# Value products cut into 64-key halves with two sums, and other work moved around the last slots

## The chip, the cores and the metric

The kernel runs on one core of one Trainium2 chip. The metric is the time of one execution on the device, in microseconds (us). The kernel before took 841.43 us (median of 3 runs, 840.59 to 842.06). The engines are called as in the profile: PE (matmul), PEld (its weight loads), DVE, ACT, POOL, and SP, which here only issues transfers (DMA).

## The reference

```python
def _A_ref(x, wqkv, wo):             # S = 2048, D = 512, H = 32, Dh = 16, W = 256
    q, k, v = ...                    # x @ wqkv, by heads
    scores = jnp.einsum("bhqd,bhkd->bhqk", q, k) * (Dh ** -0.5)
    mask = (idx[:, None] - idx[None, :] >= 0) & (idx[:, None] - idx[None, :] < W)
    p = _softmax(jnp.where(mask[None, None], scores, -1e9), axis=-1)
    o = jnp.einsum("bhqk,bhkd->bhqd", p, v)
    return o.reshape(B, S, D) @ wo   # after moving heads behind positions

def _B_ref(x, w_gate, w_up, w_down): # F = 1792
    return (_silu(x @ w_gate) * (x @ w_up)) @ w_down

g = _sigmoid((x * gate_w).sum(-1, keepdims=True))
return g * _A_ref(...) + (1 - g) * _B_ref(...)
```

Everything is float32. Each query sees itself and the 255 keys before it. The result is a gated mix of attention over that window and a feed-forward block (SwiGLU).

## The kernel before, in words

Large products are done as three products of split operands: a matrix is split into a rounded part and a rest (`split`, L64 to L67: the rounded part by ACT, POOL or DVE, the rest by POOL or DVE), and hi·hi, lo·hi and hi·lo are summed in PSUM. Scores use the split too; the value products (L320) are plain float32 and go through PE in two passes each.

The program is written out in order by hand (`manual_schedule`), so each engine executes its instructions in the order of the code. It has three stages.

*Start.* x is split, the value projection and the query and key projections of the first head group are done.

*Slots.* There are 8 groups of 4 heads and 16 blocks of 128 positions, so 128 slots `t`, and one more at the end (L524). A slot goes through four heads `hd`. For each, PE computes one score tile of the next group (L265), whose row maximum DVE takes (L267), and one score tile of this group (L302), which ACT exponentiates into `pt` (L304); POOL cuts the window's edges (L306, L309). Between them stand six matmuls of 64 rows (L216), two at a time in the upper and lower half of the array. They belong to *units*: four slots make a unit, which projects queries and keys of a later group or computes a tile of the gate and up products of the feed-forward block. Results go from PSUM (`pa`, `pb`, two buffers each) to SBUF by ACT copies (L474), and feed-forward tiles go on to DRAM (`raws`) by SP. A table `AT` puts further functions behind a head of a slot (`later`).

*In the first slot of a unit, at head 1*, comes `av`: the value products of the 512 queries `c` of a group that have just been completed. For each of up to six key blocks of 128 there are four products, one for each head, in four lanes of 32 columns; the `vg` tile is the weight (16 values and a column of ones), `pt` is streamed, and the lanes write four row groups of one PSUM tile (`pb`, at the end `pa`). Then `evac` transposes that tile in blocks of 32 on DVE (L330), and the generator `finish` divides by the sum (L336, L337), transposes back (L341) and writes to DRAM (`od`, issued by POOL), one step a slot at head 1. Just ahead of `av`, where a maximum of half a group is due, `put_max` transposes it on PE (L277), negates it on DVE (L279) and puts it into `QT`.

*The last group.* From slot 112 (`g7`) there are no scores of a next group, and so no maxima. There the gate sums of x · gate_w are done on DVE (L507), two blocks in each odd slot from 113, and down-projection weights are loaded and split for the first eight tiles (`wd_early`). The sigmoid's rest (L559 to L562) is done behind the slots.

*Down products.* For each of 4 column blocks `c` and 14 tiles `n`, `hidden` takes gate and up tiles back from DRAM (`load_kept`, L619 to L623, names `got`), applies SiLU on ACT and multiplies on DVE (L638); tile n = 1 is computed on PE instead (L634). `halved` splits the result into `hh` (ACT, L64) and `hl` (DVE, L67), and `step` does 12 matmuls (L82 to L84: three products for each of four accumulators `ps`). Further down weights are fetched and split on DVE eight tiles ahead, from n = 0 on. The attention's output projection and the mix stand among these steps.

What decides about memory: a pool that is opened later takes the SBUF of one that was closed, and the first transfer into it waits for every user of the old one.

Of the kernel before, what the change touches and what calls it, by code (L numbers as in the profile page):

```python
# [9 lines left out]
F32 = mybir.dt.float32  # L10
# [23 lines left out]
def gated_mix(ctx, tc, xT, xn, wqk, wv, wo, wgu, wd, gw, out):  # L34
# [43 lines left out]
    def mm3(ps, pairs, start=True, stop=True):  # L78

        n = len(pairs)  # L80
        for i, ((lh, ll), (rh, rl)) in enumerate(pairs):
            nc.tensor.matmul(ps, lh, rh, start=start and i == 0, stop=False)  # L82
            nc.tensor.matmul(ps, lh, rl, start=False, stop=False)  # L83
            nc.tensor.matmul(ps, ll, rh, start=False, stop=stop and i == n - 1)  # L84

    def run(gen, n=None):

# [77 lines left out]
    with ExitStack() as A:  # L165
# [107 lines left out]

        def put_max(g, hf):
            n = NB // 2
            pt = ps1.tile([P, CH], F32, name="ps1")
            nc.tensor.transpose(pt[:4 * n, :P], MX[g, hf].rearrange("p h b -> p (h b)"), ident)  # L277
            mt = sm.tile([4 * n, P], F32R, name="mt")
            nc.vector.tensor_scalar(mt, pt[:4 * n, :P], -1.0, None, op0=ALU.mult)  # L279
            for pr in range(2):  # L280
                nc.sync.dma_start(halves_of(QT[g % 2][pr])[hf][63::64].bitcast(F32),
                                  mt[2 * pr * n:2 * (pr + 1) * n].bitcast(F32))
# [30 lines left out]

        def av(g, c):

            AV[g, c] = pp.tile([P, CH], F32, name="pb" if 4 * g + c + 1 < len(UNITS) else "pa")
            for kb in range(max(0, 4 * c - 2), 4 * c + 4):
                b0, b1 = max(kb, 4 * c), min(kb + 3, 4 * c + 4)
                for j in range(4):
                    nc.tensor.matmul(AV[g, c][32 * j:32 * j + 32, (b0 - 4 * c) * P:(b1 - 4 * c) * P],  # L320
                                     VG[4 * g + kb // 4][:, kb % 4, 17 * j:17 * j + 32],
                                     PT[g, kb, j // 2][:, j % 2, (b0 - kb) * P:(b1 - kb) * P],
                                     start=kb == max(0, 4 * c - 2), stop=kb == 4 * c + 3, skip_group_check=True)

        OT = {}

        def evac(g, c):

            OT[g, c] = osb.tile([P, CH], F32, name="ot")
            nc.vector.transpose(OT[g, c], AV[g, c])  # L330

        def finish(g, c):

            v = OT[g, c].rearrange("p (s e) -> p s e", e=32)
            rc = osb.tile([P, CH // 32], F32, name="rc")
            nc.vector.reciprocal(rc, v[:, :, DH])  # L336
            nc.vector.tensor_tensor(out=v[:, :, :DH], in0=v[:, :, :DH],  # L337
                                    in1=rc[:, :, None].to_broadcast([P, CH // 32, DH]), op=ALU.mult)
            yield
            on = osb.tile([P, CH], F32, name="on")  # L340
            nc.vector.transpose(on, OT[g, c])  # L341
            yield
            nc.gpsimd.dma_start(od[g, :, c * CH:(c + 1) * CH], on)

        vp = ExitStack()
        vpool = vp.enter_context(tc.tile_pool(name="vpool", bufs=1))
        wvh = vpool.tile([P, NK, D], F32R, name="wvh")
        wvl = vpool.tile([P, NK, D], F32R, name="wvl")
        vs = [vpool.tile([P, G, 2, VW], F32, name=f"vs{i}") for i in range(2)]
# [102 lines left out]
        for n in range(4):  # L452
            load_v(n)
        vp.close()
        ptp = A.enter_context(tc.tile_pool(name="ptp", bufs=13))
        osb = A.enter_context(tc.tile_pool(name="osb", bufs=1))


        AT = {}

        def later(t, hd, *fs):
            AT.setdefault((t, hd), []).extend(fs)
# [1 line left out]
        def unit(key, t):  # L464


            later(t, 3, prepare)

            def done(hf):
                def copies(ps):  # L470
                    t0 = t + 3 + hf
                    places = [kept(), kept()]
                    for m in range(2):
                        later(t0, 2 * m, lambda m=m: nc.scalar.copy(places[m], ps[m]))  # L474
                    if key[0] == "f":
                        for m in range(2):
                            later(t0 + 1, 2, lambda m=m: nc.sync.dma_start(raws[key[1], key[2], 2 * hf + m], places[m]))
                        return
                    g = key[1]

                    def half(m):
                        if m == 0:
                            X[g, hf] = x_pair()
                        split_qk(g, hf, m, places[m])
                    t1 = t0 + 3 * hf
                    later(t1, 3, lambda: half(0))
# [23 lines left out]
        def wd_early(t, f, piece):  # L510
            later(t, 2, lambda: later(t + 1, 2, load_wd(f, piece, kept())))

        pieces = [h for two in (QT[0], KT[0], QT[1], KT[1]) for t in two for h in halves_of(t)]
        later(g7, 1, gate_place)
        for m in range(NB // 2):
            for b in (2 * m, 2 * m + 1):
                later(g7 + 2 * m, 1, lambda b=b: gate_fetch(b))
                later(g7 + 2 * m + 1, 3 * (b % 2), lambda b=b: gate_block(b))
            wd_early(g7 + 2 * m, ORDER[m], pieces[m])

        FIN, tops = iter(()), [(0, 1)]
        for t in range(G * NB + 1):  # L524
# [6 lines left out]
            for hd in range(4):  # L531
# [5 lines left out]
                run(turns[part], 3)  # L537
                for f in AT.pop((t, hd), ()):
                    f()
                if hd == 1 and part:  # L540
                    run(FIN, 1)
                if hd == 1 and part == 0:
                    while tops:
                        put_max(*tops.pop())
                    if t:
                        ag, c = divmod(d - 1, NCH)
                        av(ag, c)
                        evac(ag, c)
                        FIN = finish(ag, c)
            if i in (7, 15) and g + 1 < G:  # L550
                tops.append((g + 1, i // 8))
            if t >= 10 and t % 4 == 2 and t + 6 < G * NB:
                load_v((t + 6) // 4)
        prepare()
        run(FIN)
        for key in sorted(AT):
            for f in AT[key]:
                f()
        nc.scalar.activation(gate, gate, AF.Exp, scale=-1.0)  # L559
        nc.vector.tensor_scalar(gate, gate, 1.0, None, op0=ALU.add)  # L560
        nc.vector.reciprocal(gate, gate)
        nc.vector.tensor_scalar(igate, gate, -1.0, 1.0, op0=ALU.mult, op1=ALU.add)  # L562


    with ExitStack() as B:
        hp = B.enter_context(tc.tile_pool(name="hp", bufs=3))
        got = B.enter_context(tc.tile_pool(name="got", bufs=4))
# [26 lines left out]
        def attn_out(c, b, ohl):  # L594
# [4 lines left out]
            if c == 0:  # L599
                put(c, b, pa, gate)  # L600
            else:
                nc.scalar.activation(GA[:, b], pa, AF.Copy, scale=gate[:, t:t + 1])

        def put(c, b, ps, factor):

            t = 4 * c + b
            nc.vector.scalar_tensor_tensor(GA[:, b], ps, factor[:, t:t + 1], GA[:, b], op0=ALU.mult, op1=ALU.add)
            nc.sync.dma_start(out[0, t * P:(t + 1) * P], GA[:, b])

        def attn_step(c, b, hold={}):  # L610

# [5 lines left out]
        GOT = {}  # L617

        def load_kept(c, f):  # L619

# [23 lines left out]
            split(hh, hl, sg, nc.scalar, nc.vector)  # L644
            return c, n, hh, hl

        ACC = {}
        GA = by_k(slot("k11", F32))

        def step(c, n, hh, hl):  # L650

# [5 lines left out]
            if n == NF - 1:  # L657
                for b in range(4):
                    t = 4 * c + b
                    if c == 0:  # L660
                        nc.scalar.activation(GA[:, b], ACC[c][b], AF.Copy, scale=igate[:, t:t + 1])
# [4 lines left out]
        loads = [(c, ORDER[n]) for c, n in seq if n != 1]  # L666
        for _ in range(3):
            load_kept(*loads.pop(0))
        fresh, waiting, ready = [], [], []
        for c, n in seq:  # L670
            f = ORDER[n]
            todo, ready = ready, []
            if c == 0 and n < NF - 8:
                ready.append(load_wd(ORDER[n + 8], pieces[n + 8], raw2()))
            if c == 0 and n >= 6 and n % 2 == 0:
                ready.append(load_wo((n - 6) // 2))
            if n != 1 and loads:
                load_kept(*loads.pop(0))
            fresh.append((c, n, hidden(c, f)))
            for f in todo:  # L680
                f()
            while len(fresh) > (c + n > 0):
                waiting.append(halved(*fresh.pop(0)))
            if c == 0 and n >= NF - 4:
                load_oc(0, n - NF + 4)
            if c and 1 <= n < 5:
# [44 lines left out]
```

## Time and profile before

| what | value |
|---|---|
| median of 3 runs | 841.43 us (840.59 to 842.06) |
| the profiled execution's own time | 840.66 us |
| its span in the trace | 838.9 us |
| instructions | 18738 |
| value products (L320), matmul passes | 1408 |
| score exponentials (L304) | 512, mean 476 ns |
| score maxima (L267) | 512, mean 540 ns |
| end of slots, start of down products | about 608 to 618 us |

A row of a group reads: line, engine, operation, output <- inputs, partitions x elements, count | busy time in us, mean ns of one | idle time of the engine ahead of it, and what ended it. `128*32` is an array tile of 128 rows and 32 columns. A row of the chain of work reads: start in us, us, what. A row of the timeline reads: start, us, what, and in brackets the idle time ahead of it with its releaser. In a view of windows each engine's busy time and its count follow the length, then the granted PE clock, the share of the DMA engines and GB/s. PE matmuls overlap in the trace, so the mean of one is longer than its distance from the next.

### The profile page before, as it was taken

How to read it: one execution, taken by the hardware profiler on the slowest of the kernel's cores; microseconds unless marked ns; L12 is line 12 of the kernel's file. 1: busy time of each engine (PE TensorE's matmuls, PEld its weight loads, DVE VectorE, ACT ScalarE, POOL GpSimd, SP SyncE). 2: the span in 40 equal slices, each digit the busy share in tenths (PEclk: the TensorE clock that was granted, in tenths of full speed). 3: DMA queues.
4: the chain of work that ended last, by engine and by line, in shares of the span. 5: the costliest groups of instructions: out<-in, count | busy, mean ns of one | idle time of the engine just before them, and what ended most of it. 6: DMA issues, size and time to landing. Idle time of an engine off the chain costs nothing.

```text
span 838.9 us, 18738 instructions
## 1 busy us (share of the span) xinstructions
PE 829.5 (99%) x6934; PEld 682.2 (81%) x6934; DVE 504.9 (60%) x1380; ACT 433.9 (52%) x903; POOL 352.4 (42%) x638
## 2 busy tenths in 40 slices
PE   9999999999999999999999999999989999999998
PEld 7798878888878887887887788878858888888886
DVE  6396676677667666676677667746467353353443
ACT  6322656556656666566565665556544433243341
POOL 7712545455546555545554645456601111011020
PEclk9999999999999999999999999999999999999999
DMA  8573534625624533542552463456688444283451
GB/s 288 162 231 113 149 120 123 186 93 148 198 87 129 151 135 111 163 153 98 152 182 93 123 184 125 132 189 198 232 283 298 157 155 162 85 283 98 151 163 50
DMA packets 65996, 132.82 MB, mean 158 GB/s; under 512 B 9457, under 2 KB 14193, under 8 KB 65905
## 3 DMA queue, kind: packets, MB, share of 16 engines
q1 hardware_dynamic: 61936, 117.74, 44.6%
q0 software_dynamic: 3968, 13.90, 4.6%
q8 instruction: 54, 0.88, 0.4%
q14 instruction: 38, 0.30, 0.1%
HBM read 60.82 MB, written 45.35 MB: 127 GB/s over the span
## 4 chain that ended last, share of the span: by engine, by line
PE 96%; DMA 2%; SPq 1%; DVE 1%; issue 0%; ACT 0%
PE pb L216 24%; PE pa L216 23%; PE pb L320 9%; PE ps L84 6%; PE ps L265 6%; PE ps L82 6%; PE ps L83 6%; PE ps L302 5%; PE pb L196 2%; PE pa L196 2%; PE pb L84 2%; PE pb L83 2%; PE pb L82 2%; PE pb L634 1%; PE pa L634 1%; DMA raw<-wd 1%
## 5 line engine op out<-in xcount | busy, mean ns | idle before, releaser
L304 ACT ACTIVATE pt<-ps 128x384 f32<-128x384 f32 (+2 forms) x512 | 240.1, 476 | 210.6 <-PE ps L302 151.2
L267 DVE CUSTOM_DVE_ANT_0 ps<-ps,mask 128x384 f32<-128x384 f32 (+2 forms) x512 | 273.0, 540 | 90.3 <-PE ps L265 64.4
L306 POOL TENSOR_SCALAR_AFFINE_SELECT pt<-pt 128x256 f32<-128x256 f32 x256 | 113.8, 445 | 238.7 <-ACT pt L304 238.6
L302 PE MATMUL ps<-q,k 64*128 64x384 f32 (+2 forms) x512 | 160.2, 329 | 0.0
L265 PE MATMUL ps<-k,q 63*128 63x384 f32 (+2 forms) x512 | 159.0, 330 | 0.3 <-issue 0.3
L216 PE MATMUL pb<-xhi,wh 64*128 64x512 f32 x512 | 111.1, 394 | 0.0
L216 PE MATMUL pa<-xhi,wh 64*128 64x512 f32 x512 | 110.2, 393 | 0.0
L216 PE MATMUL pb<-xhi,wl 64*128 64x512 f32 x512 | 109.8, 389 | 0.0
L216 PE MATMUL pb<-xlo,wh 64*128 64x512 f32 x512 | 109.7, 390 | 0.0
L216 PE MATMUL pa<-xhi,wl 64*128 64x512 f32 x512 | 108.9, 390 | 0.0
L216 PE MATMUL pa<-xlo,wh 64*128 64x512 f32 x512 | 108.8, 390 | 0.0
L265 PEld LDWEIGHTS ps<-k,q 63*128 63x128 f32 x512 | 89.3, 184 | 13.7 <-issue 6.0
L302 PEld LDWEIGHTS ps<-q,k 64*128 64x128 f32 x512 | 89.3, 184 | 7.6 <-issue 0.8
L309 POOL TENSOR_SCALAR_AFFINE_SELECT pt<-pt 128x256 f32<-128x256 f32 x224 | 94.5, 422 | 0.0
L638 DVE TENSOR_TENSOR sg<-got,sg 128x512 f32<-128x512 f32 x52 | 44.0, 846 | 64.0 <-ACT sg L637 52.6
L320 PE MATMUL pb<-pt,vg 128*32 128x256 f32 (+2 forms) x1360 | 81.5, 386 | 0.0
L320 PEld LDWEIGHTS pb<-pt,vg 128*32 128x32 f32 x1360 | 40.1, 110 | 41.0 <-issue 21.4
L267 DVE DVE_READ_ACCUMULATOR2_ANT mx<- 128x1 f32 x512 | 72.2, 141 | 0.0
L330 DVE STREAM_TRANSPOSE ot<-pb 128x512 f32<-128x512 f32 x31 | 22.2, 717 | 77.7 <-PE pb L320 77.7
L216 PEld LDWEIGHTS pb<-xhi,wh 64*128 64x128 f32 x512 | 56.8, 185 | 7.4
L216 PEld LDWEIGHTS pb<-xhi,wl 64*128 64x128 f32 x512 | 56.9, 184 | 6.5
L216 PEld LDWEIGHTS pa<-xhi,wl 64*128 64x128 f32 x512 | 55.8, 184 | 7.0
(144 smaller groups left out, 1483.4 us busy)
## 6 DMA issues: line engine op xcount, KB each, us to landing
raws<-ev SPq DMA_DIRECT2D x104, 256.0 KB
got<-raws SPq DMA_DIRECT2D x104, 256.0 KB
od<-on POOLq DMA_DIRECT2D x32, 256.0 KB, 2.4
raw<-wgu SPq DMA_DIRECT2D x28, 256.0 KB
q<-xhi SPq DMA_DIRECT2D x56, 128.0 KB
k<-xhi SPq DMA_DIRECT2D x56, 128.0 KB
vd<-vs POOLq DMA_DIRECT2D x8, 672.0 KB, 4.5
vg<-vd SPq DMA_DIRECT2D x32, 168.0 KB
```

The costliest lines, as they stand in the source:

```text
L82: nc.tensor.matmul(ps, lh, rh, start=start and i == 0, stop=False)
L83: nc.tensor.matmul(ps, lh, rl, start=False, stop=False)
L84: nc.tensor.matmul(ps, ll, rh, start=False, stop=stop and i == n - 1)
L216: mm = nc.tensor.matmul(ps[me], w[r], x[r], start=not second and i == 0, stop=bool(second) and i == n - 1)
L265: nc.tensor.matmul(ps[:, :n], QT[g % 2][pr][r, q0:q0 + P], KT[g % 2][pr][r, k0:k0 + n], start=True, stop=True)
L267: mx = nc.vector.tensor_tensor_reduce(out=ps[:, :n], in0=ps[:, :n], in1=mask[:, 3 * P - n:], scale=1.0, scalar=NEG, op0=ALU.add, op1=ALU.m ...
L302: nc.tensor.matmul(ps[:, :n], KT[g % 2][pr][r, k0:k0 + P], QT[g % 2][pr][r, k0:k0 + n], start=True, stop=True)
L304: BEHIND.append(nc.scalar.activation(pt[:, j, :n], ps[:, :n], AF.Exp, scale=SCALE))
L306: nc.gpsimd.affine_select(out=pt[:, :, :P], in_=pt[:, :, :P], pattern=[[0, 2], [1, P]], compare_op=ALU.is_ge, fill=0.0, base=0, channel_mu ...
L309: nc.gpsimd.affine_select(out=pt[:, :, 2 * P:], in_=pt[:, :, 2 * P:], pattern=[[0, 2], [-1, P]], compare_op=ALU.is_ge, fill=0.0, base=-1, ...
L320: nc.tensor.matmul(AV[g, c][32 * j:32 * j + 32, (b0 - 4 * c) * P:(b1 - 4 * c) * P], VG[4 * g + kb // 4][:, kb % 4, 17 * j:17 * j + 32], PT ...
L638: nc.vector.tensor_tensor(out=sg, in0=gu[1], in1=sg, op=ALU.mult)
```

## The change

1. *Value products by halves of 64 keys.* `av` cuts each key block into its lower and upper 64 keys, and both have their own row half of the array: eight lanes of 64 rows and 32 columns. The sum over lower halves goes to `pb` (or `pa`), that over upper halves to a tile of `ps2`, or of `ps1` from the last group on. The blocks are taken in two orders so that both halves are equally wide in each round.
2. *Two sums.* `finish` copies the second sum on ACT, adds both on DVE, transposes, divides, transposes back and writes. Its first step stands behind `av`, the next behind head 2 of the same slot, the others behind head 1 of the next three slots. `evac` is gone.
3. `put_max` transposes in two halves, each into its own PSUM tile, by plain matmuls of 64 rows.
4. *Gate sums* start in slot 108, one behind head 2 and one behind head 3 of every odd slot; the sigmoid's rest stands in slot 125.
5. *The first tail tile* (c = 0, n = 0) is loaded in slot 124 and multiplied and split in slot 128, head 0, into half of `KT[1][1]`.
6. *Down rows* are loaded six tiles ahead, from n = 2 on, and their split stands behind `halved`.
7. The pools of value weights, `pt`, tail tiles (`hp`) and `got` are put on the right side of SBUF, and the ACT copies at the very end both stand at head 0.

```diff
         def put_max(g, hf):
             n = NB // 2
-            pt = ps1.tile([P, CH], F32, name="ps1")
-            nc.tensor.transpose(pt[:4 * n, :P], MX[g, hf].rearrange("p h b -> p (h b)"), ident)
             mt = sm.tile([4 * n, P], F32R, name="mt")
-            nc.vector.tensor_scalar(mt, pt[:4 * n, :P], -1.0, None, op0=ALU.mult)
+            for o in HALVES:
+                pt = ps1.tile([P, CH], F32, name="ps1")
+                nc.tensor.matmul(pt[:4 * n, :64], MX[g, hf].rearrange("p h b -> p (h b)")[o], ident[o, o],
+                                 start=True, stop=True)
+                nc.vector.tensor_scalar(mt[:, o], pt[:4 * n, :64], -1.0, None, op0=ALU.mult)
...
-            AV[g, c] = pp.tile([P, CH], F32, name="pb" if 4 * g + c + 1 < len(UNITS) else "pa")
-            for kb in range(max(0, 4 * c - 2), 4 * c + 4):
-                b0, b1 = max(kb, 4 * c), min(kb + 3, 4 * c + 4)
+            AV[g, c] = (pp.tile([P, CH], F32, name="pb" if 4 * g + c + 1 < len(UNITS) else "pa"),
+                        ps1.tile([P, CH], F32, name="ps1") if 4 * g + c + 1 >= 4 * (G - 1) else ps2.tile([P, CH], F32, name="ps2"))
+            orders = [[4 * c + m for m in ms if 4 * c + m >= 0] for ms in ((0, 1, 2, -1, -2, 3), (0, 1, -1, 2, 3, -2))]
+            for n, kbs in enumerate(zip(*orders)):
                 for j in range(4):
-                    nc.tensor.matmul(AV[g, c][32 * j:32 * j + 32, (b0 - 4 * c) * P:(b1 - 4 * c) * P],
-                                     VG[4 * g + kb // 4][:, kb % 4, 17 * j:17 * j + 32],
-                                     PT[g, kb, j // 2][:, j % 2, (b0 - kb) * P:(b1 - kb) * P],
-                                     start=kb == max(0, 4 * c - 2), stop=kb == 4 * c + 3, skip_group_check=True)
+                    for h, (o, kb) in enumerate(zip(HALVES, kbs)):
+                        k0 = kb * P + 64 * h
+                        q0, q1 = max(k0, c * CH), min(k0 + W + 64, c * CH + CH)
+                        nc.tensor.matmul(AV[g, c][h][32 * j:32 * j + 32, q0 - c * CH:q1 - c * CH],
+                                         VG[4 * g + kb // 4][o, kb % 4, 17 * j:17 * j + 32],
+                                         PT[g, kb, j // 2][o, j % 2, q0 - kb * P:q1 - kb * P],
+                                         start=n == 0, stop=n == len(orders[0]) - 1, skip_group_check=True)
...
         def finish(g, c):
-            v = OT[g, c].rearrange("p (s e) -> p s e", e=32)
+            first, second = AV[g, c]
+            if not AB:
+                AB.extend(osb.tile([P, CH], F32, name=f"o{n}") for n in range(2))
+            both, ot = AB[::-1] if c % 2 else AB
+            lo = 0 if c else 64
+            nc.scalar.copy(both[:, lo:], second[:, lo:])
+            yield
+            nc.vector.tensor_tensor(out=both[:, lo:], in0=first[:, lo:], in1=both[:, lo:], op=ALU.add)
+            if lo:
+                nc.vector.tensor_copy(both[:, :lo], first[:, :lo])
+            yield
+            nc.vector.transpose(ot, both)
+            yield
...
-        later(g7, 1, gate_place)
+        later(g7 - 4, 1, gate_place)
+        for b in range(NB):
+            t = g7 - 4 + b // 2 * 2
+            later(t, 1, lambda b=b: gate_fetch(b))
+            later(t + 1, 2 + b % 2, lambda b=b: gate_block(b))
+        later(g7 + NB - 3, 0, gate_end)
...
+        def tile0():
+            (gt, up), sg = [GOT.pop((ORDER[0], i, 0)) for i in range(2)], kept()
+            nc.scalar.activation(sg, gt, AF.Silu)
+            nc.vector.tensor_tensor(out=sg, in0=up, in1=sg, op=ALU.mult)
+            split(*TILE0, sg, nc.scalar, nc.vector)
+        later(g7 + NB - 4, 1, tile0_load)
+        later(g7 + NB - 1, 3, lambda: later(g7 + NB, 0, prepare, tile0))
...
-                if hd == 1 and part:
+                if (part, hd) in ((0, 2), (1, 1), (2, 1), (3, 1)):
                     run(FIN, 1)
...
                         av(ag, c)
-                        evac(ag, c)
                         FIN = finish(ag, c)
+                        run(FIN, 1)
...
-        fresh, waiting, ready = [], [], []
+        fresh, waiting, ready = [], [(0, 0, *TILE0)], []
...
-            if c == 0 and n < NF - 8:
-                ready.append(load_wd(ORDER[n + 8], pieces[n + 8], raw2()))
+            if c == 0 and 2 <= n < NF - 6:
+                ready.append(load_wd(ORDER[n + 6], pieces[n + 6], raw2()))
...
-            fresh.append((c, n, hidden(c, f)))
+            if c + n:
+                fresh.append((c, n, hidden(c, f)))
+            if len(fresh) > 1:
+                waiting.append(halved(*fresh.pop(0)))
             for f in todo:
                 f()
-            while len(fresh) > (c + n > 0):
-                waiting.append(halved(*fresh.pop(0)))
```

On PE, the value products of the second block of 512 queries of group 0 stood in this order (the line, the operation, out<-in, the columns of the array by the columns streamed):

```order
L216 MATMUL pa<-xhi_71,wl 128x512
L277 MATMUL ps_1559<-ident,mx 32x128
L320 MATMUL pb<-pt,vg 32x128 x4
L320 MATMUL pb<-pt,vg 32x256 x4
L320 MATMUL pb<-pt,vg 32x384 x8
L320 MATMUL pb<-pt,vg 32x256 x4
L320 MATMUL pb<-pt,vg 32x128 x4
L265 MATMUL ps_1592<-k_353,q_351 128x384
```

In the changed kernel the same place on PE begins and goes on as follows, with both sums in turn (eight rows of each width but 320, of which there are sixteen):

```order
L218 MATMUL pa<-xhi_71,wl 128x512
L281 MATMUL ps_1586<-ident,mx 32x64
L281 MATMUL ps_1589<-ident,mx 32x64
L330 MATMUL pb<-pt,vg 32x320
L330 MATMUL ps_1595<-pt,vg 32x320
...
L330 MATMUL pb<-pt,vg 32x256
...
L330 MATMUL pb<-pt,vg 32x192
...
L330 MATMUL pb<-pt,vg 32x64
...
L330 MATMUL pb<-pt,vg 32x128
L330 MATMUL ps_1595<-pt,vg 32x128
L267 MATMUL ps_1645<-k_353,q_351 128x384
```

The 24 products have become 48, each over 64 keys, and the widest is 320 instead of 384.

On DVE, behind those products, before (ISA is the score maximum and the reading of its result):

```order
L279 TENSOR_SCALAR mt<-ps_1559 32x128
L330 STREAM_TRANSPOSE ot<-pb 128x512
L267 ISA ps_1592,mx<-ps_1592,mask 128x384
L267 ISA mx 128x1
...
L336 RECIPROCAL rc<-ot 128x16
L337 TENSOR_TENSOR ot<-ot,rc 128x16x16
```

and with the change (`o` are the two tiles that `finish` uses in turn):

```order
L283 TENSOR_SCALAR mt<-ps_1586 32x64
L283 TENSOR_SCALAR mt<-ps_1589 32x64
L269 ISA ps_1645,mx<-ps_1645,mask 128x384
L269 ISA mx 128x1
L347 TENSOR_TENSOR o_1336<-pb,o_1336 128x512
```

The reader of `pb` has moved behind the maximum of the next head, and is an addition that also waits for ACT's copy.

Where the down products begin, DVE had this order before (`sg` SiLU times up, `hl` the rest of its split, `q` the place of a down-weight tile, `raw` the tile as loaded):

```order
L638 TENSOR_TENSOR sg_9873<-got1_9857,sg_9873 128x512
L67 TENSOR_TENSOR hl_9877<-sg_9873,hh_9876 128x512
L638 TENSOR_TENSOR sg_9908<-pb_9895,sg_9908 128x512
L66 CAST q10_350<-raw2_9867 128x512
L67 TENSOR_TENSOR q10_350<-raw2_9867,q10_350 128x512
L638 TENSOR_TENSOR sg_9919<-got1_9861,sg_9919 128x512
L66 CAST q10_350<-raw2_9880 128x512
L67 TENSOR_TENSOR q10_350<-raw2_9880,q10_350 128x512
L67 TENSOR_TENSOR hl_9925<-sg_9908,hh_9924 128x512
```

and with the change:

```order
L559 TENSOR_TENSOR ev_10571<-k11_353,ev_10571 128x512
L67 TENSOR_TENSOR k11_353<-ev_10571,k11_353 128x512
L347 TENSOR_TENSOR o1_1336<-pa_10576,o1_1336 128x512
...
L676 TENSOR_TENSOR sg_10697<-pb_10684,sg_10697 128x512
L676 TENSOR_TENSOR sg_10706<-got1_10657,sg_10706 128x512
L67 TENSOR_TENSOR hl_10710<-sg_10697,hh_10709 128x512
L676 TENSOR_TENSOR sg_10735<-got1_10661,sg_10735 128x512
L67 TENSOR_TENSOR hl_10739<-sg_10706,hh_10738 128x512
L66 CAST q10_350<-raw2_10700 128x512
L67 TENSOR_TENSOR q10_350<-raw2_10700,q10_350 128x512
```

The first tile (its two rows, into `k11`) now stands ahead of the last value product's addition, and the second tile's `hl` ahead of the first split of down weights, not behind two of them.

More of the change, by code (lines that the diff above doesn't have):

```diff
@@ L84, in mm3 @@
             nc.tensor.matmul(ps, ll, rh, start=False, stop=stop and i == n - 1)
+    HALVES = slice(0, 64), slice(64, P)
     def run(gen, n=None):
@@ L319, in av @@
+            for n, kbs in enumerate(zip(*orders)):
                 for j in range(4):
-                    nc.tensor.matmul(AV[g, c][32 * j:32 * j + 32, (b0 - 4 * c) * P:(b1 - 4 * c) * P],
-                                     VG[4 * g + kb // 4][:, kb % 4, 17 * j:17 * j + 32],
-                                     PT[g, kb, j // 2][:, j % 2, (b0 - kb) * P:(b1 - kb) * P],
-                                     start=kb == max(0, 4 * c - 2), stop=kb == 4 * c + 3, skip_group_check=True)
-        OT = {}
@@ L327, in evac @@
-        def evac(g, c):
-            OT[g, c] = osb.tile([P, CH], F32, name="ot")
-            nc.vector.transpose(OT[g, c], AV[g, c])
-        def finish(g, c):
-            v = OT[g, c].rearrange("p (s e) -> p s e", e=32)
+                    for h, (o, kb) in enumerate(zip(HALVES, kbs)):
[5 more added lines that the diff above has]
+                                         start=n == 0, stop=n == len(orders[0]) - 1, skip_group_check=True)
@@ new lines, in gated_mix @@
+        AB = []
+        def finish(g, c):
+            first, second = AV[g, c]
[11 more added lines that the diff above has]
+            yield
+            v = ot.rearrange("p (s e) -> p s e", e=32)
@@ L339, in finish @@
             yield
-            on = osb.tile([P, CH], F32, name="on")
-            nc.vector.transpose(on, OT[g, c])
+            nc.vector.transpose(both, ot)
+            nc.gpsimd.dma_start(od[g, :, c * CH:(c + 1) * CH], both)
             yield
-            nc.gpsimd.dma_start(od[g, :, c * CH:(c + 1) * CH], on)
         vp = ExitStack()
-        vpool = vp.enter_context(tc.tile_pool(name="vpool", bufs=1))
+        vpool = vp.enter_context(tc.tile_pool(name="vpool", bufs=1, side="right"))
         wvh = vpool.tile([P, NK, D], F32R, name="wvh")
@@ L454, in gated_mix @@
         vp.close()
-        ptp = A.enter_context(tc.tile_pool(name="ptp", bufs=13))
+        ptp = A.enter_context(tc.tile_pool(name="ptp", bufs=13, side="right"))
         osb = A.enter_context(tc.tile_pool(name="osb", bufs=1))
-        AT = {}
+        AT, GOT = {}, {}
         def later(t, hd, *fs):
@@ L473, in copies @@
                     for m in range(2):
-                        later(t0, 2 * m, lambda m=m: nc.scalar.copy(places[m], ps[m]))
+                        later(t0, 2 * m if t0 < G * NB else 0, lambda m=m: nc.scalar.copy(places[m], ps[m]))
                     if key[0] == "f":
@@ L511, in wd_early, with gate_end, tile0_load @@
             later(t, 2, lambda: later(t + 1, 2, load_wd(f, piece, kept())))
-        pieces = [h for two in (QT[0], KT[0], QT[1], KT[1]) for t in two for h in halves_of(t)]
-        later(g7, 1, gate_place)
+        def gate_end():
+            nc.scalar.activation(gate, gate, AF.Exp, scale=-1.0)
+            nc.vector.tensor_scalar(gate, gate, 1.0, None, op0=ALU.add)
+            nc.vector.reciprocal(gate, gate)
+            nc.vector.tensor_scalar(igate, gate, -1.0, 1.0, op0=ALU.mult, op1=ALU.add)
+        pieces = [h for two in (QT[0], KT[0], QT[1], KT[1]) for t in two for h in halves_of(t)]
+        later(g7 - 4, 1, gate_place)
[4 more added lines that the diff above has]
+        later(g7 + NB - 3, 0, gate_end)
         for m in range(NB // 2):
-            for b in (2 * m, 2 * m + 1):
-                later(g7 + 2 * m, 1, lambda b=b: gate_fetch(b))
-                later(g7 + 2 * m + 1, 3 * (b % 2), lambda b=b: gate_block(b))
             wd_early(g7 + 2 * m, ORDER[m], pieces[m])
+        TILE0 = halves_of(halves_of(KT[1][1])[1])
+        def tile0_load():
+            for i, place in enumerate(halves_of(halves_of(KT[1][1])[0])):
+                GOT[ORDER[0], i, 0] = place.bitcast(F32)
+                nc.sync.dma_start(GOT[ORDER[0], i, 0], raws[ORDER[0], i, 0])
+        def tile0():
[5 more added lines that the diff above has]
+        later(g7 + NB - 1, 3, lambda: later(g7 + NB, 0, prepare, tile0))
         FIN, tops = iter(()), [(0, 1)]
@@ L553, in gated_mix @@
                 load_v((t + 6) // 4)
-        prepare()
         run(FIN)
@@ L558, in gated_mix @@
                 f()
[L559 to L562, printed above, removed]
     with ExitStack() as B:
-        hp = B.enter_context(tc.tile_pool(name="hp", bufs=3))
-        got = B.enter_context(tc.tile_pool(name="got", bufs=4))
+        hp = B.enter_context(tc.tile_pool(name="hp", bufs=3, side="right"))
+        got = B.enter_context(tc.tile_pool(name="got", bufs=4, side="right"))
         bp = B.enter_context(tc.tile_pool(name="bp", bufs=2))
@@ L601, in attn_out @@
             else:
-                nc.scalar.activation(GA[:, b], pa, AF.Copy, scale=gate[:, t:t + 1])
+                nc.scalar.activation(GA[0][:, b], pa, AF.Copy, scale=gate[:, t:t + 1])
         def put(c, b, ps, factor):
             t = 4 * c + b
-            nc.vector.scalar_tensor_tensor(GA[:, b], ps, factor[:, t:t + 1], GA[:, b], op0=ALU.mult, op1=ALU.add)
-            nc.sync.dma_start(out[0, t * P:(t + 1) * P], GA[:, b])
+            ga = GA[0][:, b]
+            nc.vector.scalar_tensor_tensor(ga, ps, factor[:, t:t + 1], ga, op0=ALU.mult, op1=ALU.add)
+            nc.sync.dma_start(out[0, t * P:(t + 1) * P], ga)
         def attn_step(c, b, hold={}):
@@ L615, in attn_step @@
                 hold[c, b] = attn_split(c, b)
-        GOT = {}
         def load_kept(c, f):
@@ L645, in halved @@
             return c, n, hh, hl
-        ACC = {}
-        GA = by_k(slot("k11", F32))
+        ACC, GA = {}, []
         def step(c, n, hh, hl):
@@ L657, in step @@
             if n == NF - 1:
+                if c == 0:
+                    GA.append(by_k(slot("k11", F32)))
                 for b in range(4):
@@ L660, in step @@
                     if c == 0:
-                        nc.scalar.activation(GA[:, b], ACC[c][b], AF.Copy, scale=igate[:, t:t + 1])
+                        nc.scalar.activation(GA[0][:, b], ACC[c][b], AF.Copy, scale=igate[:, t:t + 1])
                     else:
@@ L665, in gated_mix @@
         seq = [(c, n) for c in range(NCH) for n in range(NF)]
-        loads = [(c, ORDER[n]) for c, n in seq if n != 1]
+        loads = [(c, ORDER[n]) for c, n in seq if n != 1 and c + n]
         for _ in range(3):
             load_kept(*loads.pop(0))
-        fresh, waiting, ready = [], [], []
+        fresh, waiting, ready = [], [(0, 0, *TILE0)], []
         for c, n in seq:
```

## The prediction

> **What bounds the kernel now.** I read the page first, then the waits of the matmul engine, then the chain of work that ended last, then the timelines at the places the change touches.
>
> ```profile
> PE 829.5 (99%) x6934; PEld 682.2 (81%) x6934; DVE 504.9 (60%) x1380; ACT 433.9 (52%) x903; POOL 352.4 (42%) x638
> ...
> PE 96%; DMA 2%; SPq 1%; DVE 1%; issue 0%; ACT 0%
> PE pb L216 24%; PE pa L216 23%; PE pb L320 9%; PE ps L84 6%; PE ps L265 6%; PE ps L82 6%; PE ps L83 6%; PE ps L302 5%; PE pb L196 2%; PE pa L196 2%; PE pb L84 2%; PE pb L83 2%; PE pb L82 2%; PE pb L634 1%; PE pa L634 1%; DMA raw<-wd 1%
> ```
>
> PE is busy for 99% of the 838.9 us span, and it is 96% of the chain. So time comes off only where PE has fewer columns to stream or stops waiting. The value products (L320) are 9% of the chain. The waits of PE are few:
>
> ```profile
> PE ps L84 <- DVE hl L67: 1.9, 1, 1.9
> PE ps L82 <- ACT hh L64: 1.5, 1, 1.5
> PE pa L171 <- POOL ident masks.py:199: 1.4, 1, 1.4
> ```
>
> The first two (each: total us, times, longest) are single waits of 1.9 and 1.5 us. They lie where the slots end and the down products begin, and the chain shows what stands behind the later one:
>
> ```profile
> 616.29 5.42 DMA raw<-wd
> 621.74 0.44 DVE q L66
> 622.24 0.57 issue
> 622.81 0.70 DVE hl L67
> 623.55 0.63 PE ps L84
> 624.18 0.43 PE ps L82
> 624.61 0.43 PE ps L83
> ...
> 626.74 0.43 PE ps L82
> 627.17 0.30 PE ps L83
> 627.46 0.23 PE ps L84
> ```
>
> A down-weight load takes 5.42 us in a crowd of transfers, its split on DVE stands in front of the split of the second tail tile (hl), and PE waits for hl until 623.55. The nine matmuls from there to 627.46 then take 3.91 us where nine at 0.23 would take 2.07. In that stretch the granted clock was low (the two shares before the last number are the clock and the DMA engines):
>
> ```profile
> 623.50:627.50 4.00, 3.95 (x10) 3.12 (x11) 3.05 (x6) 1.88 (x4) 0.00 (x0) 0.57 0.91 293
> ```
>
> So the passage costs 1.9 + 1.5 us of waiting and 1.84 us of half-speed clock behind it: **5.2 us**.
>
> **The value products.** One of a later query block (24 of the 32) and one of a first block (8 of 32) stand in the chain as
>
> ```profile
> 397.12 2.73 PE pb L320 x48
> ...
> 363.95 2.08 PE pb L320 x32
> ```
>
> and by shape as (count | busy, mean ns)
>
> ```profile
> L320 PE MATMUL pb<-pt,vg 128*32 128x384 f32 x496 | 45.9, 488 | 0.0
> L320 PEld LDWEIGHTS pb<-pt,vg 128*32 128x32 f32 x1360 | 40.1, 110 | 41.0 <-issue 21.4 <-ACT ev L474 3.3 <-ACT pt L304 2.9
> ```
>
> The x48 are 24 products in two passes each, 4 column lanes at once. The timeline of weight loads inside that first one shows the pace:
>
> ```profile
> 398.05 0.13 PEld L320 LDWEIGHTS pb<-pt,vg 128*32 128x32 f32 x4 [0.19 <-issue]
> 398.37 0.13 PEld L320 LDWEIGHTS pb<-pt,vg 128*32 128x32 f32 x4 [0.19 <-issue]
> 398.70 0.13 PEld L320 LDWEIGHTS pb<-pt,vg 128*32 128x32 f32 x4 [0.19 <-POOL pt L309]
> ```
>
> Four loads of 110 ns fit in 0.13 us, so the lanes run together and start some 7 ns apart; and a round of four 384-wide passes follows the one before after 0.32 us, which is 0.833 ns a column. Checking: a lane streams 128+256+384+384+256+128 = 1536 columns, twice, times 0.833 ns = 2.56 us, and the chain has 2.73; a first block 1152 columns, 1.92, and the chain has 2.08. The 0.17 over is entry and exit.
>
> **Part 1, 64 keys at a time.** The array is cut by rows as well. A 64-key half reaches only 320 queries where 128 keys reach 384, so a lane streams 320+320+256+192+64+128 = 1280 columns instead of 1536 (first block: the wider lane 320+320+256+128 = 1024 instead of 1152). Twice 256 columns at 0.833 ns are 0.427 us less, twice 128 are 0.213 us. Against that stands the weight load: a 64-wide pass is 53 ns of streaming under a load of 110 ns, so I charge its two passes 0.114 us more. That leaves 0.313 x 24 + 0.213 x 8 = 7.5 + 1.7 = **9.2 us saved**. Bounds: 11.9 if loads hide after all (0.427 x 24 + 1.7), zero or below if the rounds don't keep this pace (rivals).
>
> That row lanes run at once is shown by the projection beside it:
>
> ```profile
> 396.26 0.39 PE L216 MATMUL pa<-xhi,wh 64*128 64x512 f32 x2
> 396.49 0.39 PE L216 MATMUL pa<-xlo,wh 64*128 64x512 f32 x2
> ```
>
> Two 64-row matmuls of 512 columns per 0.23 us. Eight lanes (rows and columns together) no row shows.
>
> The Trainium skill, "TensorE: Matmul & The Clock Gate", section "Wait — 56ns, not 53.3ns?", says that matmuls never start less than about 25 ns apart, however narrow. The loads above, four in 0.13 us at 110 ns each, start much closer in separate lanes, so I weigh it low; by the rule the sum would be 5.5 instead of 9.2 (a rival below, worked from rows).
>
> **Part 2, two sums instead of one.** New are one copy on ACT and one addition on DVE for each unit, beside the transposes and the normalising that were there. Nearest rows:
>
> ```profile
> L474 ACT COPY ev<-pb 128x512 f32<-128x512 f32 x64 | 37.4, 585 | 0.5 <-ACT ev L474 0.5
> L638 DVE TENSOR_TENSOR sg<-pb,sg 128x512 f32<-128x512 f32 x4 | 2.8, 690 | 26.7 <-PE pb L634 26.7
> ```
>
> 32 x 0.585 = 18.7 us of ACT and 32 x 0.69 = 22.1 us of DVE, on engines busy 52% and 60%. PE does not stand behind them unless a PSUM tile comes free too late. After the product that ended at 399.85:
>
> ```profile
> 399.92 0.72 DVE L330 STREAM_TRANSPOSE ot<-pb 128x512 f32<-128x512 f32 x1 [2.83 <-PE pb L320]
> 400.56 0.53 DVE L267 CUSTOM_DVE_ANT_0 ps<-ps,mask 128x384 f32<-128x384 f32 x1
> 401.01 0.13 DVE L267 DVE_READ_ACCUMULATOR2_ANT mx<- 128x1 f32 x1
> ...
> 401.99 0.57 DVE L267 CUSTOM_DVE_ANT_0 ps<-ps,mask 128x384 f32<-128x384 f32 x1 [0.24 <-PE ps L302]
> ...
> 400.35 0.49 ACT L304 ACTIVATE pt<-ps 128x384 f32<-128x384 f32 x1 [2.76 <-PE ps L302]
> ...
> 401.80 0.39 PE L216 MATMUL pb<-xhi,wh 64*128 64x512 f32 x2
> ...
> 402.66 0.39 PE L216 MATMUL pb<-xhi,wh 64*128 64x512 f32 x2
> ```
>
> Now the transpose frees pb at 400.64, and PE writes pb again at 401.80. After the change pb is free when copy (0.585) and addition (0.69) are done, with up to one score maximum (0.57 + 0.14) between them on DVE: 1.28 to 1.99 us behind the end, against 1.95 (401.80 - 399.85). DVE sat idle 0.24 us before the maximum at 401.99, so it catches up. The first exponential behind the copy moves by up to 0.585 - (400.35 - 399.92) = 0.16 us. I take 0.01 us a unit, 0.3 in all; bounds: 0, and 0.3 us for each of 32 units, 9.6 (a rival).
>
> **Part 3, gate sums from slot 108.** The blocks are moved, not added. But four of them now fall in slots 109 and 111, where score maxima still run:
>
> ```profile
> L507 DVE SCALAR_TENSOR_TENSOR xhi<-xlo,xhi 128x512 f32<-128x512 f32 x16 | 12.1, 756 | 13.8 <-DMA xlo<-xn 13.8
> L267 DVE CUSTOM_DVE_ANT_0 ps<-ps,mask 128x384 f32<-128x384 f32 x448 | 250.0, 565 | 65.5 <-PE ps L265 45.1 <-PE ps L302 19.5
> ...
> L277 PE MATMUL ps<-ident,mx 128*32 128x128 f32 x16 | 4.6, 285 | 0.0
> ```
>
> Two blocks are 1.5 us in a slot of four heads, each head 0.86 us long (401.80 to 402.66 above) with 0.71 of it taken by a maximum. Four heads leave 0.6 us. What is short, 0.9 us in each of two slots, is partly buffered by two score tiles: 1.0 us lost, bounds 0 and 1.8. Two half transposes of the maxima take the place of each of the 16 of 0.285 us (the last row). Their streaming is the same 128 columns, so I take nothing; bounds: a third of the 285 ns either way, -1.5 and +1.5 us.
>
> **Part 4, the passage to the down products.** The first tail tile is split in the slots and the down loads start at n = 2, so the first step has hh and hl before PE asks, and in the second hl no longer stands behind a wd split. Both waits should go, and with them the idle time after which the clock was 0.57: **5.2 us saved**, bounds 0 and 5.2. The SP queue at this place sheds the early wd loads, and tail tiles no longer share the DMA engines (0.91 busy above) with them. Splits moved into slot 128 lie on ACT and DVE, which have no exponentials or maxima there. What is late next is the load six steps ahead: at 12 matmuls of 0.23 us a step, six steps are 16.6 us against a load of 5.42.
>
> **The sum** for the profiled execution, 840.66 us (span 838.9 and 1.8 around it): -9.2 - 5.2 + 0.3 + 1.0 = -13.1, so 827.6. The median shown, 841.43, lies 0.8 above that execution: **828.4 us**.
>
> **Rivals.**
> 1. *PE can't issue that fast (slower).* A later block now needs 48 products x 2 passes x 2 (load and matmul) = 192 instructions in 2.41 us, 12.6 ns each; before, 96 in 2.73, 28 ns each. No row shows a sustained rate below that. All value products have 24 x 192 + 8 x 128 = 5632 instructions, planned at 24 x 2.42 + 8 x 1.87 = 73.0 us. The other terms and the 9.2 give 13.1 us to lose, so from (73.0 + 13.1) / 5632 = 15.3 ns an instruction the kernel is no faster; at 18 ns it takes 857 us, at 20 ns 868. For it: twice the instructions with narrower work. Against it: four loads, with matmuls between, start within about 20 ns.
> 2. *The eight lanes don't run together* (the change doesn't do what it says). Then row halves take turns: 2 x 2 x 1280 x 0.833 = 4.26 us + 0.17 against 2.73, and 3.2 + 0.17 against 2.08, 51 us more, 889 us. Against it: rows pair at L216 and columns in fours at L320.
> 3. *A floor on matmul starts.* At 25 ns between starts, 96 matmuls take 2.4 + 0.17 us: 0.16 saved instead of 0.31, the first blocks unchanged: 24 x 0.16 + 1.7 = 5.5, 832 us. That floor is the one the Trainium skill states in the section named above.
> 4. *Copy and addition are waited for*: 0.3 us a unit, 9.3 more, 838 us. For it: the 1.99 against 1.95 above. Against it: idle DVE and ACT each head.
> 5. *The passage waits elsewhere* (tile loads in place of weight splits): 3 to 5 us come back, 832 to 834 us. For it: 0.91 DMA share; against it: fewer bytes there.
>
> **How the numbers follow.** Forecast 0.52 (824 to 831), rival 1 0.13, rival 2 0.03, rival 3 0.11, rival 4 0.11, rival 5 0.10. A measurement of this kernel can tell about 0.2%, 1.7 us, from no change. Faster: forecast, 3, 5, most of 4 and none of 1 and 2: 0.81. Same: the end of 4 and the part of 1 near 15 ns: 0.05. Slower: 0.14. The range 823 to 840 holds the forecast, 3, 4 and 5, and leaves out rival 1 and 2 and a little below (loads fully hidden).
>
> **What would show it.** In the profile after: the chain's value products at 2.4 and 1.85 us (step 1; 2.7 or more means rivals 1 to 3, and the distance of load starts tells which); PE's waits on a pb tile or a score tile behind ACT or DVE (step 2, rival 4) and near slot 109 (step 3); no wait of L84 and L82 at the passage and a granted clock near 1 there (step 4). A low clock without a wait, or a rate of issue that can't be sustained, would make the prediction wrong.

## The result and the profile after

The changed kernel takes 834.27 us (median of 6 runs, 833.73 to 836.09), the kernel before 840.52 us (6 runs): a ratio of 0.9925, interval 0.9912 to 0.9938. That is 6.2 us saved where 13.1 had been worked out. The profiled execution (836.09 us, span 834.0) is the highest of the six.

The page of the changed kernel, its busy times and the shares of the chain:

```profile
PE 826.3 (99%) x8390; PEld 698.6 (84%) x8390; DVE 516.4 (62%) x1436; ACT 448.5 (54%) x935; POOL 351.7 (42%) x638
...
PE 94%; DMA 3%; DVE 1%; ACT 1%; issue 0%; SPq 0%; POOL 0%; DVEq 0%; ACTq 0%
PE pb L218 24%; PE pa L218 24%; PE pb L330 6%; PE ps L267 6%; PE ps L84 5%; PE ps L82 5%; PE ps L83 5%; PE ps L306 5%; PE ps L330 2%; PE pa L198 2%; PE pb L198 2%; PE pb L84 2%; PE pb L83 2%; PE pb L82 2%; DMA raw<-wd 1%; PE pb L672 1%
```

PE is as full as before, so waiting is not where the missing time went. Its waits (total, times, longest) say the same:

```profile
PE pa L173 <- POOL ident masks.py:199: 1.4, 1, 1.4
PE pa L198 <- ACT xhi L64: 1.2, 2, 0.7
PE ps L267 <- DVE mt L283: 0.3, 1, 0.3
PE ps L267 <- issue: 0.3, 1, 0.3
PE pa L198 <- DVE xlo L67: 0.2, 1, 0.2
PE ps L84 <- DVE hl L67: 0.2, 1, 0.2
```

The 1.9 us and 1.5 us at the passage are down to 0.2 us in all. New is a wait at the very start (L198 on xhi). The chain of the changed kernel, and then that of before, show the first load of x and the second block of projections behind it:

```profile
1.72 6.29 DMA q<-xT
...
15.58 11.20 PE pb L198 x48
```

```profile
2.19 4.83 DMA q<-xT
...
12.96 11.16 PE pb L196 x48
```

That load took 6.29 us here, and 4.71 to 5.89 us in the profiled executions of e1 to e7 below. The kernel of e1 has the same start and reaches the first unit's matmuls at 35.1 us, as the kernel before did (35.2); this execution reaches them at 37.9. So the 2.7 us belong to this execution, not to the change.

Next the value products, by the timeline of weight loads (start, us). The block shown is the second later block of a group, in the changed kernel and then before.

```profile
395.83 0.10 PEld L330 LDWEIGHTS pb<-pt,vg 64*32 64x32 f32 x1 [0.37 <-ACT pt L308]
...
398.31 0.18 PEld L267 LDWEIGHTS ps<-k,q 63*128 63x128 f32 x1 [0.20 <-issue]
```

```profile
397.05 0.81 PEld L320 LDWEIGHTS pb<-pt,vg 128*32 128x32 f32 x24 [0.36 <-ACT ev L474]
...
399.78 0.18 PEld L265 LDWEIGHTS ps<-k,q 63*128 63x128 f32 x1 [0.20 <-issue]
```

From the first load to the first one behind them, 2.73 us have become 2.48. If the row halves took turns, it would be 4.43 (rival 2), so the eight lanes do run together.

Subtracting start times gives a table by stage (profiled executions, us, change against before):

| stage | planned | changed kernel |
|---|---|---|
| to the first unit's matmuls (35.2 us) | 0 | +2.7 (the first load) |
| from there to the first value product | 0 | +0.7 |
| first to last value product | -9.2 + 1.3 | -7.5 |
| behind the last value product | -5.2 | -0.8 |
| span | -13.1 | -4.9 |

So the slots as a whole gave nearly what was planned (-7.5 against -7.9), and the part behind them did not, though almost no wait is left there (0.2 us). What is different is the pace of the down products. The same line, 12 matmuls apart (one step; the next streams another place), in the timeline of PE, changed kernel and then before:

```profile
614.89 0.39 PE L82 MATMUL ps<-q,hh 128*128 128x512 f32 x1
...
617.69 0.39 PE L82 MATMUL ps<-q,hh 128*128 128x512 f32 x1
```

```profile
630.25 0.39 PE L82 MATMUL ps<-q,hh 128*128 128x512 f32 x1
...
632.97 0.39 PE L82 MATMUL ps<-k,hh 128*128 128x512 f32 x1
```

2.80 us against 2.72: 0.2333 us a matmul against 0.2267. Two windows of the changed kernel, the passage and a stretch behind it, exclude the clock (the granted clock is the third number from the end):

```profile
611.00:631.00 20.00, 20.00 (x88) 16.10 (x87) 15.55 (x28) 8.17 (x15) 1.79 (x2) 1.00 0.90 311
640.00:680.00 40.00, 40.00 (x174) 32.38 (x174) 19.40 (x23) 16.72 (x30) 7.58 (x6) 1.00 0.66 200
```

Over some 660 down products 6.7 ns each are 4.4 us, which is what is missing in that stage (5.2 - 0.8). The matmuls of the output projection between them (into pb) kept 0.2267 in the same kernel, with the same shapes. What the change did to the one kind and not to the other is the start address of its weights: `hp`, the pool of hh and hl, went to the right side of SBUF, where the tiles of the built program start 224 bytes past a multiple of 256; before, they started at a multiple of 256, and the output projection's operands do so in both kernels. That is theory A. Theory B is that transfers and splits in a new order beside PE, or the right side itself, slow it.

### The profile page after: what moved, and what is told of

The parts are those of the page before. It is cut to its first block, busy times and chain, and to the rows that moved or that the text cites. A ratio compares the mean times of both kernels' runs of the same rounds, so it can differ in the third digit from the quotient of the medians.

```text
span 834.0 us, 21664 instructions
## 1 busy us (share of the span) xinstructions
PE 826.3 (99%) x8390; PEld 698.6 (84%) x8390; DVE 516.4 (62%) x1436; ACT 448.5 (54%) x935; POOL 351.7 (42%) x638
## 4 chain that ended last, share of the span: by engine, by line
PE 94%; DMA 3%; DVE 1%; ACT 1%; issue 0%; SPq 0%; POOL 0%; DVEq 0%; ACTq 0%
PE pb L218 24%; PE pa L218 24%; PE pb L330 6%; PE ps L267 6%; PE ps L84 5%; PE ps L82 5%; PE ps L83 5%; PE ps L306 5%; PE ps L330 2%; PE pa L198 2%; PE pb L198 2%; PE pb L84 2%; PE pb L83 2%; PE pb L82 2%; DMA raw<-wd 1%; PE pb L672 1%
## 5 line engine op out<-in xcount | busy, mean ns | idle before, releaser
L218 PE MATMUL pb<-xhi,wh 64*128 64x512 f32 x512 | 112.9, 394 | 0.0
L218 PE MATMUL pb<-xlo,wh 64*128 64x512 f32 x512 | 111.8, 391 | 0.0
L218 PE MATMUL pb<-xhi,wl 64*128 64x512 f32 x512 | 111.6, 390 | 0.0
L676 DVE TENSOR_TENSOR sg<-got,sg 128x512 f32<-128x512 f32 x51 | 45.8, 899 | 68.4 <-ACT sg L675 64.0
L330 PE MATMUL ps<-pt,vg 64*32 64x320 f32 (+4 forms) x1408 | 75.9, 346 | 0.0
L330 PE MATMUL pb<-pt,vg 64*32 64x320 f32 (+3 forms) x1360 | 75.3, 350 | 0.0
L330 PEld LDWEIGHTS pb<-pt,vg 64*32 64x32 f32 x1360 | 48.6, 106 | 20.2 <-ACT pt L308 5.1
L218 PEld LDWEIGHTS pb<-xhi,wl 64*128 64x128 f32 x512 | 58.7, 185 | 5.7
```

The lines of the kernel that those rows point to most:

```text
L218: mm = nc.tensor.matmul(ps[me], w[r], x[r], start=not second and i == 0, stop=bool(second) and i == n - 1)
L330: nc.tensor.matmul(AV[g, c][h][32 * j:32 * j + 32, q0 - c * CH:q1 - c * CH], VG[4 * g + kb // 4][o, kb % 4, 17 * j:17 * j + 32], PT[g, kb, ...
L676: nc.vector.tensor_tensor(out=sg, in0=gu[1], in1=sg, op=ALU.mult)
```

## The experiments

**e1: tail tiles aligned.**

```diff
+        B.enter_context(tc.tile_pool(name="pad", bufs=1, side="right")).tile([P, 56], F32, name="pad")
         hp = B.enter_context(tc.tile_pool(name="hp", bufs=3, side="right"))
```

> The changed kernel with 224 unused bytes ahead of the tail pools on the right side, so that sg, hh, hl and got start at a multiple of 256 bytes (before the change they did; with it they start 224 bytes past one). Theory A (start address of the weights read by the down products): their distance goes back from 0.2335 to 0.2267 us, about 660 x 6.7 ns = 4.4 us, 829.9 us. Theory B (the slower pace comes from what runs beside it, transfers and splits in a new order, or from lying on the right side at all): distance and time stay, 834.3 us.

829.87 us (4 runs; before on this chip 841.18; ratio 0.9866, 0.985 to 0.9883). The timeline of PE:

```profile
612.13 0.39 PE L82 MATMUL ps<-q,hh 128*128 128x512 f32 x1
...
614.85 0.39 PE L82 MATMUL ps<-q,hh 128*128 128x512 f32 x1
```

That is 2.72 us again for 12. With 224 unused bytes the kernel is 4.4 us faster, as A expected, and its tiles still lie on the right side with the transfers in the changed order. Behind the last value product it now saves 4.5 us; PE still waits 0.7 us for `hl` there.

**e2: the kernel before, shifted.**

```diff
+        B.enter_context(tc.tile_pool(name="pad0", bufs=1)).tile([P, 8], F32, name="pad0")
         hp = B.enter_context(tc.tile_pool(name="hp", bufs=3))
+        B.enter_context(tc.tile_pool(name="pad1", bufs=1)).tile([P, 56], F32, name="pad1")
```

> The kernel before with the tail pool hp (sg, hh, hl) moved up by 32 bytes and nothing else. Theory A: the down products slow to 0.2335 us from 0.2267, 672 of them, 4.5 us more, 845.0 us. Theory B: 840.5 us, no change.

844.9 us (ratio 1.0044, 1.0029 to 1.0059). The slow pace appears in a kernel that has no other part of the change:

```profile
640.26 0.40 PE L82 MATMUL ps<-k,hh 128*128 128x512 f32 x1
...
643.06 0.40 PE L82 MATMUL ps<-k,hh 128*128 128x512 f32 x1
```

That is 2.80 us for 12, and 3.7 us more in all where 4.5 were expected. The kernel of e1 has all that B blames and is fast; this one has none of it and is slow. Together they settle A.

**e3: x aligned too.**

```diff
+    gate = const.tile([P, NB], F32, name="gate")
+    igate = const.tile([P, NB], F32, name="igate")
     xhi, xlo = [], []
...
-    gate = const.tile([P, NB], F32, name="gate")
-    igate = const.tile([P, NB], F32, name="igate")
```

> e1 with the two small gate tiles (128 bytes together) ahead of the split x instead of behind it, so that the streamed x parts start at a multiple of 256 bytes instead of 128 past one. Theory A, taken to the streamed operand: the pairs of 64-row matmuls go from 0.2317 us to 0.2267, 1536 pairs x 5 ns = 7.7 us, and the full-row products of x some 1.1 us more: 821.1 us. Rival: only the weights' start matters, or the pairs are paced by something else: like e1, 829.9 us.

829.75 us, like e1: the 8.8 us are not there. But the rival is only half right. Chain of e3, then of e1:

```profile
24.07 10.90 PE pa L198 x48
```

```profile
24.03 11.15 PE pa L198 x48
```

The 48 projections with 128 rows did get faster, 0.2271 us each against 0.2323. The pairs with 64 rows, by far the most, stayed: the mean distance from a pair's start to the next pair's is about 231.5 ns in both kernels. Something else paces them, and these runs don't show what.

**e6 and e7: which bytes count.** Both are the kernel before; pools are moved by unused bytes as in e2: `hp` by 64 and `wop` (woh and wol, streamed by the output products) by 32 in e6, `hp` by 128 and `bp` (oh and ol, their weights) by 96 in e7.

> The kernel before with hp moved by 64 bytes (weights of the down products) and wop by 32 (the streamed operand woh, wol of the attention's output products). If the weights have to start at a multiple of 64 bytes: down products at 0.227 us. If at a multiple of 128 or 256: 0.232 or more. If the streamed start doesn't count, as in e3: the output products stay at 0.227 us; if it does: 0.232 or more, 1.2 us.

> The kernel before with hp moved by 128 bytes and bp (oh and ol, the weights of the output products) by 96. 64 bytes as the unit: down products 0.227 us, output products 0.232 or more. 256 as the unit: both slow. Time 840 to 842 by the first, 845 to 846 by the second.

These took 846.96 and 845.06 us, one execution each, so only their paces are used here. Timeline of e6, output products, nine matmuls apart, and the same in the kernel before:

```profile
673.22 0.39 PE L82 MATMUL pb<-woh,oh 128*128 128x512 f32 x1
...
675.32 0.39 PE L82 MATMUL pb<-woh,oh 128*128 128x512 f32 x1
```

```profile
671.21 0.39 PE L82 MATMUL pb<-woh,oh 128*128 128x512 f32 x1
...
673.25 0.39 PE L82 MATMUL pb<-woh,oh 128*128 128x512 f32 x1
```

That is 2.10 us against 2.04: a streamed operand 32 bytes off is as slow as a weight that is off. All kernels together (mean distance of neighbouring matmuls in ns, from the traces, without the few distances of 260 ns or more, which hold waits; the starts are bytes past a multiple of 256 in the built programs):

| matmuls | weights | streamed | ns |
|---|---|---|---|
| down products, before / e1 | 0 | 0 | 226.8 / 226.9 |
| down products, changed | 224 | 0 | 233.2 |
| down products, e2 | 32 | 0 | 233.2 |
| down products, e6 | 64 | 0 | 233.2 |
| down products, e7 | 128 | 0 | 233.4 |
| output products, before | 0 | 0 | 226.7 |
| output products, e6 | 0 | 32 | 232.5 |
| output products, e7 | 96 | 0 | 233.8 |

My guess of 64 bytes as the unit was wrong. Of the starts tried, only multiples of 256 are fast.

**e4: the value products alone** (with the two sums and the halved transposes; all else as before).

> The kernel before with only the value products by 64 keys, their two sums and the halved maximum transposes. From the starts of the value products in the two traces the slots gain 7.5 us: 833.0 us, with the waits and the low clock at the passage kept. If the slots' gain depended on the moved pools or gate sums, less: 835 to 838 us.

835.92 us (ratio 0.9938, 0.9924 to 0.9952). That is 5.3 us saved and 2.9 us above the expected time. In the slots the gain is there (from the first value product's start to the last one's end 7.5 us less), but the waits of PE at the passage grew:

```profile
PE ps L82 <- ACT hh L64: 3.9, 1, 3.9
PE ps L84 <- DVE hl L67: 1.5, 2, 1.3
```

They are 5.4 us, against 3.4 before. The first tail tile is loaded later: 3.4 us behind the last value product's end (603.84), where it was 1.1 us before (610.59, then 611.69). The timelines of ACT and SP in e4, and what SP waited for ahead of that load:

```profile
603.87 0.59 ACT L345 COPY o<-ps 128x512 f32<-128x512 f32 x1 [1.85 <-PE ps L330]
604.36 0.59 ACT L492 COPY ev<-pb 128x512 f32<-128x512 f32 x1
...
600.91 4.39 SPq L495 DMA_DIRECT2D raws<-ev  x3
607.21 2.74 SPq L641 DMA_DIRECT2D got<-raws  x6
...
SPq L641 <- DMA raws<-ev: 1.6, 1, 1.6
```

In the kernel before, ACT did the same copy while the last value products ran:

```profile
607.94 1.08 ACT L474 COPY ev<-pb 128x512 f32<-128x512 f32 x2 [0.50 <-ACT ev L474]
```

By the trace it is the copy of the second sum, then, that delays the passage: on ACT it waits for the last value product, and the last feed-forward copy (604.36) stands behind it. That copy's result goes to DRAM from 604.98 on, and SP waits for its landing before it loads the first tail tile. The chain of work names DVE's division ahead of this load, which ended at 607.11; but SP's 1.6 us went to the store, and the division only ended at the same moment. The changed kernel has both feed-forward copies ahead of the sum's (item 7 of the change), and its loads begin at 606.57, 0.07 us behind its last value product.

**e5: the rest of the change alone** (the products, transposes and finishing steps of before put back).

> The changed kernel with the value products, the maximum transposes and the finishing steps of before: what is left of the change are the gate sums, the first tail tile in the slots, the down rows six ahead, and the pools on the right side (hh and hl 224 bytes past a multiple of 256). Theory A (start address): the passage's 5.2 us saved, 4.4 us given back by slower down products: 840.0 us, with no wait of L84 or L82 and a pace of 0.233 us in the trace. Rival: the passage was not worth 5.2 us in the first place and nothing is given back: also near 840, but with the pace of before, 0.227 us.

840.61 us against 841.26 (ratio 0.9995, 0.9984 to 1.0006): no difference that can be told. The waits at the passage are gone but for 0.6 us, and the pace is the slow one, as theory A expected:

```profile
PE ps L84 <- DVE hl L67: 0.6, 1, 0.6
```

```profile
639.92 0.40 PE L82 MATMUL ps<-q,hh 128*128 128x512 f32 x1
...
642.02 0.39 PE L82 MATMUL ps<-q,hh 128*128 128x512 f32 x1
```

That is 2.10 us for nine. So a gain and a loss of 4 to 5 us stand in one change and hide each other. The value products of slot 112 begin 0.46 us later than in the kernel before (547.51 against 547.05), those of slot 108 as before (530.36 against 530.40). PE falls behind near 540 us (the same matmul starts at 540.26 before and at 540.70 here), where the two gate sums of slot 109 stand among the score maxima; slot 111 adds nothing. That is the price of the gate sums.

**e8: e1 with the second sum of slot 112 in ps2.**

```diff
-ps1.tile([P, CH], F32, name="ps1") if 4 * g + c + 1 >= 4 * (G - 1) else
+ps1.tile([P, CH], F32, name="ps1") if 4 * g + c + 1 > 4 * (G - 1) else
```

> e1 with the second sum of the value products of slot 112 in ps2 and not in ps1. In the changed kernel these products take 2.96 us against 2.57 of their like; the theory is that they wait there for the two ps1 tiles of the maximum transposes just ahead. If so: 2.57 us, the wait of L267 on the negated maxima (0.3 us) gone, 829.5 us. Rival: they wait for the last exponentials or masks, and the length stays 2.9 us.

829.76 us (ratio 0.986, 0.9846 to 0.9874), no different from e1. These products go from 2.94 us in e1 (540.66 to 543.60, first load to the next score's) to 2.49 (541.02 to 543.51), but PE then waits elsewhere, a wait that e1 has not:

```profile
PE ps L306 <- ACT o L345: 0.3, 1, 0.3
```

A score tile of ps2 now stands behind the copy of the sum. Of the 0.45 us, some 0.3 are lost again. The other half of the theory fell: the 0.3 us on negated maxima remain. They lie at 83.8 us, at the second halved transpose, not in slot 112.

## Why the prediction was half right

- **Value products.** The mechanism was right, and so was the first block's size: 0.20 us saved (planned 0.21). A later block without a transpose ahead saves 0.25 (planned 0.31), one with a transpose ahead 0.18, and the one of slot 112 loses 0.23. The sum over all 32 lengths is 5.9 us. Another 1.5 us went between the blocks, nearly all where a halved transpose stands ahead, for which I had taken nothing. Together that is 7.4 in place of 9.2; the runs don't show why a later block keeps 0.06 us and a halved transpose saves time.
- **Eight lanes, issue, the 25 ns floor.** Rivals 1 to 3 are out: a later block takes 2.48 us. The first and the eighth matmul of the block shown above, in PE's timeline of the changed kernel:

```profile
395.83 0.45 PE L330 MATMUL pb<-pt,vg 64*32 64x320 f32 x1
...
395.88 0.45 PE L330 MATMUL ps<-pt,vg 64*32 64x320 f32 x1
```

  Eight starts within 0.05 us are some 7 ns from one to the next. The floor of about 25 ns that the Trainium skill gives in "TensorE: Matmul & The Clock Gate", section "Wait — 56ns, not 53.3ns?", does not hold between lanes here. Whether it holds in one lane no run here shows.
- **Copy and addition.** In the slots they cost nothing that shows, against 0.3 planned and rival 4's 9.3. Where the copy did cost is a place that I had not looked at, behind the last product: 2.0 us (e4). In the changed kernel nothing of it is left, with the last feed-forward copies ahead of it and the first tail tile ready early; no run separates these two.
- **Gate sums.** 1.0 us planned, 0.46 in e5. In the changed kernel the way from slot 108's products to slot 112's is only 0.16 us longer than in e4, which has the gate sums of before.
- **Start.** The first two halved transposes, near 65 and 83 us, where no value products run yet, cost some 0.6 us together; I had bounded them by 1.5 and taken 0.
- **The passage.** The waits and the low clock went as forecast: 5.2 us planned, 4.5 saved in e1, where 0.7 us of waiting for `hl` is left.
- **What failed** is the premise that "time comes off only where PE has fewer columns to stream or stops waiting", and with it the sum: "-9.2 - 5.2 + 0.3 + 1.0 = -13.1" has no term for the pools on the right side. I listed them as part of the change and took a tile's place as free, so every matmul that was not touched kept its pace. They cost 4.4 us in the down products by their pace and by the median of e1 (3.7 by e2). With that undone the kernel takes 829.87 us, 1.5 above the forecast of 828.4.
- **Luck.** The measured 834.27 lies inside the range of 823 to 840 because the range made room for rivals 3, 4 and 5, and none of them came. It lies beside rival 5's "832 to 834", but the waits of that rival are not there. The low pace was none of the five rivals, and the signs I named, waits and clock, could not have shown it. The slots' total, too, is nearer to the plan than its terms, because the smaller gain of the products and the smaller costs of the gate sums and copies offset each other.

## What to carry to other kernels

When a change moves pools, compare the start addresses of matmul operands before and after, not only whether they fit. When a stage loses time with PE busy, no wait and a full clock, compare the distance of equal matmuls between two traces: 6.7 ns times some hundreds was two fifths of what this change could bring. A part that measures as "no difference" can hold a gain and a loss of the same size, so undo its pieces one by one.

## What the runs showed of the hardware

In executions with a mean granted clock of 0.997 to 1.0, split-float32 matmuls of 128 rows and 512 columns followed each other after some 226.7 ns where weights and streamed operand both started at a multiple of 256 bytes. They took 232.3 to 233.8 ns where one of the two started off it: the weights by 32, 64, 96, 128 or 224 bytes, or the streamed operand by 32 (e6) or 128 (e1 against e3). Why is not shown. Two kinds of matmul did not follow this. Pairs of 64 rows took about 231.5 ns with x at 128 (e1) and at 0 (e3). Plain float32 value products took 2.48 us a later block with the streamed pt at 224 bytes (changed kernel) and at 0 (e4); that says nothing of their weights, most of which start off a multiple of 256 in both kernels, 17 columns of `vg` apart. Eight array tiles of 64 rows by 32 columns work at once, with loads and matmuls of different tiles starting some 7 ns apart.
